# Spreading the first inversion over the preparation, in an RWKV-7 kernel with a top-k mixture behind it

## The chip, the cores and the metric

The kernel runs on one core of a Trainium2 chip. The metric is the device time of one execution in microseconds (us), as the median of several runs. The engines are TensorE (PE), VectorE (DVE), ScalarE (ACT), GpSimd (POOL) and SyncE (SP, which here only issues DMAs). Line numbers (L456) are those of the kernel before.

## The reference

Two blocks, one behind the other, in float32. The first is a recurrence over 768 time steps for 4 batches and 8 heads of 40 features:

```python
for t in range(S):
    y[:, :, t] = np.einsum('bhd,bhde->bhe', rt, state)
    Sa = np.einsum('bhde,bhe->bhd', state, at)
    state_decay = state * wt[:, :, None, :] - np.einsum('bhd,bhe->bhde', Sa, bt)
    state = state_decay + np.einsum('bhd,bhe->bhde', vt, kt)
```

The second block takes the 3072 rows of y (320 features), gives each to the best of 8 experts, keeps the 80 with the largest gate for each expert, and multiplies those by two matrices with a ReLU between.

## The kernel before, in words

**Units.** The sequence is cut into 12 chunks of 64 steps; a unit is one chunk of two batches with their eight heads, so there are 24 units. Within a chunk the recurrence is solved at once: a triangular system of 64 rows for each head and batch. Its two diagonal blocks of 32 rows are inverted explicitly; all the inversions of four units (a group) lie side by side on the 128 partitions, and one inversion handles a group.

**Preparation of a unit n**, eight units ahead of its use (`AHEAD = 8`):

- `decays` turns w on TensorE and copies it out on ACT; `forward` (L291) and `backward` (L298) are DVE's running products of it; `doubled` (L312) is a copy on POOL into `qd`.
- `turned_a` and `decayed_a` (L307) turn a on TensorE and scale it on DVE.
- `inverted` (L324, L326) turns `qd` and scales the keys and b with it on DVE: `scaled`. Behind it the next unit's keys and b are loaded into the single buffer `raw_s`.
- `operand` (L336) turns `scaled` into `sT`. `qd` and `sT` share one buffer: both are tiles of tag "turn" in a pool that has one of each tag.
- `system` (L259) multiplies `ahT` by `sT` in 64 small matmuls; `system_kept` (L346) copies the result to `nt` on ACT and writes its diagonal blocks to DRAM (`blocks`); `psi_masked` (L265) masks it on POOL.

**Inversion of a group k.** `fetch` reads the four units' blocks back in another layout (`lt`, four DMAs, L361). `begin` (L366) fills `tt` from it on POOL. Then come 30 steps (`step`, L377 and L380), each a product and a sum on DVE, of 30 to 240 elements on 128 partitions. `end` writes `tt` to DRAM (`solved`, L383), `returned` reads it back in the layout of the units (`dt`, four DMAs, L390). `diagonal` (L456) multiplies with `dt` on TensorE, twice for each unit.

**Recurrence.** The main loop has one iteration n for each unit. It finishes unit n - 1 (`turned`, `lower` with its masks on POOL, `summed`, L521, with the state update, L524), computes unit n (`together`, `right`, `diagonal` 0, `reads_g`, `below`, `turned_r`, `diagonal` 1), and prepares unit n + 8 and part of unit n + 9. The inversion of group n // 4 + 1 begins at n % 4 = 0 and its steps are spread over four iterations.

**Order.** All of this is written out by hand: `do` chains the instructions of each engine in the order of the calls, DMAs by the engine that issues them. `pause(steps, us)` emits inversion steps until their estimated costs have used up the given us. The queue for a-loads and for one of the k-loads is ACT's during the preparation, and SP's from the line `queues[1] = nc.sync` on; all other DMAs named here are SP's.

**Before the loop**, units 0 to 5 are prepared in a row, then the inversion of group 0 runs (with the rest of unit 5 beside its first steps), then units 6 and 7 are prepared and 8 is begun.

Of the kernel before, what the change touches and what calls it, by code (L numbers as in the profile page):

```python
# [8 lines left out]
F32 = mybir.dt.float32  # L9
# [9 lines left out]
def kernel(  # L19
# [32 lines left out]
    T = 64  # L52
    C = 32
    NS = T // C
    Z = 2
# [3 lines left out]
    G = H // 2  # L59
    NM = NC * BP  # L60

    NG = 4
# [83 lines left out]
    with ExitStack() as p1:  # L146
# [5 lines left out]
        sb = p1.enter_context(tc.tile_pool(name="sb", bufs=1))  # L152
# [176 lines left out]
                    in1=ps[q][:, :, :, 0:D], op=Alu.mult)  # L329
            load(n + 1, "s")  # L330

        def operand(n):
            t = sb.tile([128, G, Z, 2, T], F32, name="sT", tag="turn")
            of[n]["sT"] = sT = t.rearrange("p g z i t -> p (g z i t)").rearrange("p (z g s) -> p z g s", z=Z, g=G)
            for p, m in zip(by_half(of[n]["s"]), halves):
                nc.scalar.copy(sT[:, :, :, m], p)  # L336

# [363 lines left out]
        def pause(todo, us_):  # L701
            while todo and us_ > 0:
                cost, f = todo.pop(0)
                do(f)
                us_ -= cost

        def invert(k):
            steps.extend(((i * (C - 1 - i) * 1.04 + 155) * 2e-3, lambda i=i: step(k, i)) for i in range(1, C - 1))

        def joined(n):  # L710
            do(operand, n)
            do(system, n)
            do(system_kept, n)
            do(psi_masked, n)

        def prepare(n, before=None, next_=True):


            do(turned_a, n)
            do(decayed_a, n)  # L720
            if next_:
                do(decays, n + 1)
            if next_:
                do(forward, n + 1)
            do(inverted, n)
            if before is not None:
                do(operand, before)
                do(system, before)
                do(system_kept, before)
                do(psi_masked, before)  # L730
            if next_:
                do(backward, n + 1)
                do(doubled, n + 1)

        def started(n):
            do(decays, n)
            do(forward, n)
            do(backward, n)
            do(doubled, n)

        do(load, 0, "was")
        started(0)
        prepare(0)
        for n in range(1, NG + 1):
            prepare(n, n - 1)
        do(fetch, 0)
        do(begin, 0)
        do(load, 0, "rv")
        prepare(NG + 1, NG, False)
        invert(0)  # L750
        pause(steps, 5)
        joined(NG + 1)
        do(load, 1, "v")
        do(load, 2, "v")
        pause(steps, 100)
        do(end, 0)
        do(returned, 0)
        queues[1] = nc.sync
        started(NG + 2)
        prepare(NG + 2)  # L760
        prepare(NG + 3, NG + 2)
        prepare(NG + 4, NG + 3, False)
        do(fetch, 1)
        do(operand, NG + 4)

        waiting, turn, inverting = [], None, None

# [3 lines left out]
        for n in range(NU + 2):  # L771
# [41 lines left out]
            pause(steps, 0.4)  # L813
            if n == NU:
                pause(rounds_, 2)
            if n % NG == 0 and n + NG < NU:
                inverting = n // NG + 1
                do(begin, inverting)
                invert(inverting)
# [12 lines left out]
            if now:  # L832
                do(reads_g, n)
                do(below, n)
            pause(steps, (3.5, 5.3, 5.3, 100)[n % NG] if coming else (6.5, 9, 100, 100)[n % NG])
            pause(rounds_, LISTS.get(n, 0))
            back = None
            if inverting and not steps:
                do(end, inverting)
                back, inverting = inverting, None  # L840
# [4 lines left out]
                turn = None  # L845
            if now:
                do(turned_r, n)
            if coming and m % NG == NG - 1:
                do(fetch, m // NG)
            if back:  # L850
                do(returned, back)
            if now:
                do(reads_r, n)
                do(diagonal, n, 1)
# [225 lines left out]
```

## Time and profile before

| | us |
|---|---|
| median of 3 runs (625.06 to 629.06) | 628.08 |
| the profiled execution's own time | 625.24 |
| its span in the profile | 623.5 |
| TensorE busy / DVE / ACT / POOL | 480.9 / 370.2 / 218.4 / 187.0 |
| first step of the first inversion, end of its last | 65.25, 88.9 |
| first multiplication with `dt` (L456) | 126.84 |
| state updates of units 0 and 21 (L524) | 153.82, 482.56 |

In the timeline a row has the start, the duration, the engine and line, what is written from what, and in brackets how long the engine had been idle and what ended that. Rows of "SPq" are DMA issues, whose duration is the time that issuing takes, not that of the transfer. PEclk in the slices is the granted clock of TensorE in tenths. In the list of groups the last column is the idle time just before these instructions, with its main releaser.

### The profile page before, as it was taken

What the parts mean: (1) busy time and instruction counts of PE and PEld (TensorE: products, weight loads), DVE (VectorE), ACT (ScalarE), POOL (GpSimd) and SP (SyncE); (2) the same over time, 40 slices, a digit from 0 to 9 for tenths busy, and PEclk for the clock granted to TensorE, in tenths of its full rate; (3) what the DMA queues carried; (4) which work ended last, traced back from release to release, by engine and by line L of the source; (5) the groups of instructions that cost most, each with busy time, mean ns of one, the idle gap of its engine ahead of it and who ended that gap; (6) DMA issues with size and microseconds to landing.
All of it is one profiled execution on the core that took longest, in us unless ns stands there. A gap on an engine that the chain in (4) does not pass through costs nothing. (4 is left out here: it accounts for less than half of the span.)

```text
span 623.5 us, 25223 instructions
## 1 busy us (share of the span) xinstructions
PE 480.9 (77%) x11184; PEld 410.3 (66%) x11184; DVE 370.2 (59%) x870; ACT 218.4 (35%) x417; POOL 187.0 (30%) x277
## 2 busy tenths in 40 slices
PE   3566204797996998699988999779998830899996
PEld 2455203677885887588877788668887720787874
DVE  8533784178963698469955892587657888201010
ACT  1232201353562555455554364244554400000000
POOL 5221200223343344424444344223322210311111
PEclk9765755596997899989997799598998975899999
DMA  4646417464567455865577425335533319899500
GB/s 74 102 91 118 94 44 96 87 115 77 98 128 125 74 95 94 154 123 97 97 139 119 89 58 115 61 76 122 111 78 77 78 23 321 258 330 329 191 14 14
DMA packets 245249, 71.45 MB, mean 115 GB/s; under 512 B 229524, under 2 KB 237972, under 8 KB 245140
## 3 DMA queue, kind: packets, MB, share of 16 engines
q1 hardware_dynamic: 219888, 62.53, 47.3%
q10 hardware_dynamic: 24484, 5.67, 4.6%
q0 software_dynamic: 768, 1.64, 0.9%
q8 instruction: 88, 1.44, 0.9%
q14 instruction: 21, 0.17, 0.1%
HBM read 51.69 MB, written 18.12 MB: 112 GB/s over the span
## 5 line engine op out<-in xcount | busy, mean ns | idle before, releaser
L380 DVE TENSOR_TENSOR tt<-tt,tmp 128x30 f32<-128x30 f32 (+9 forms) x180 | 84.4, 469 | 6.6
L377 DVE TENSOR_TENSOR tmp<-tt,lt 128x30 f32<-128x30 f32 (+9 forms) x180 | 66.0, 366 | 17.4 <-POOL tt L366 6.5
L265 POOL TENSOR_SCALAR_AFFINE_SELECT side<-side 64x1024 f32<-64x1024 f32 x46 | 53.6, 1165 | 44.5 <-ACT side L507 43.0
L223 POOL COPY apart<-state 64x320 f32<-64x320 f32 x44 | 20.1, 456 | 133.2 <-DVE state L524 132.3
L456 PE MATMUL pr<-yy,dt 32*32 32x40 f32 x1536 | 42.4, 209 | 16.3 <-DMA dt<-solved 15.6
L521 PE MATMUL yp<-side,scaled 128*64 128x128 f32 (+1 forms) x768 | 51.2, 292 | 0.6 <-DVE side L505 0.6
L456 PEld LDWEIGHTS pr<-yy,dt 32*32 32x32 f32 x1536 | 35.4, 116 | 24.3 <-issue 13.5
L238 PE MATMUL tp<-ident,raw_w 128*128 128x128 f32 x96 | 18.9, 330 | 39.9 <-DMA raw_w<-in_w_dram 39.9
L521 PEld LDWEIGHTS yp<-side,scaled 128*64 128x64 f32 x768 | 45.4, 150 | 2.5 <-DVE side L505 0.9
L265 POOL TENSOR_SCALAR_AFFINE_SELECT nt<-nt 64x512 f32<-64x512 f32 x48 | 32.2, 670 | 47.4 <-ACT nt L346 45.2
L291 DVE TENSOR_TENSOR_SCAN pt<-decay,begins 128x520 f32<-128x520 f32 x24 | 32.9, 1371 | 22.0 <-ACT decay L285 20.7
L1033 DVE TENSOR_SCALAR y<-yp,weight 80x320 f32<-80x320 f32 x8 | 4.4, 547 | 70.1 <-PE yp L1031 70.1
L312 POOL COPY qd<-qt 128x1024 f32<-128x1024 f32 x24 | 24.9, 1039 | 68.2 <-DVE qt L298 60.4
L524 DVE TENSOR_TENSOR state<-yp,pt 128x320 f32<-128x320 f32 x22 | 10.8, 489 | 56.8 <-PE yp L521 56.8
L259 PE MATMUL sp<-ahT,sT 64*64 64x64 f32 x1536 | 37.5, 249 | 6.2 <-ACT sT L336 6.0
L238 PEld LDWEIGHTS tp<-ident,raw_w 128*128 128x128 f32 x96 | 13.0, 168 | 43.4 <-issue 38.9
L285 ACT COPY decay<-tp 128x512 f32<-128x512 f32 x24 | 14.1, 588 | 73.5 <-PE tp L238 64.7
L259 PEld LDWEIGHTS sp<-ahT,sT 64*64 64x64 f32 x1536 | 32.3, 159 | 10.5 <-ACT sT L336 9.4
L326 DVE TENSOR_TENSOR scaled<-raw_s,pp 128x320 f32<-128x320 f32 x48 | 21.0, 479 | 30.5 <-PE pp L324 28.5
L1031 PE MATMUL yp<-w,hT 128*80 128x320 f32 x128 | 37.4, 439 | 0.0
L414 PE MATMUL yp<-rT,gT 64*64 64x64 f32 x768 | 28.2, 223 | 11.7 <-DVE xT L530 8.8
L336 ACT COPY sT<-tp 128x512 f32<-128x512 f32 x48 | 25.8, 589 | 29.0 <-PE tp L247 25.5
(307 smaller groups left out, 1051.3 us busy)
## 6 DMA issues: line engine op xcount, KB each, us to landing
w<-in_moe_w_dram SPq DMA_DIRECT2D x8, 1280.0 KB, 14.1
w<-in_moe_w_dram SPq DMA_DIRECT2D x8, 1024.0 KB, 16.4
blocks<-nt SPq DMA_DIRECT2D x48, 128.0 KB, 2.4
raw_w<-in_w_dram SPq DMA_DIRECT2D x48, 80.0 KB, 3.3
raw_s<-in_b_dram SPq DMA_DIRECT2D x48, 80.0 KB, 3.2
raw_r<-in_r_dram SPq DMA_DIRECT2D x48, 80.0 KB, 2.9
side<-in_v_dram SPq DMA_DIRECT2D x48, 80.0 KB, 2.6
x_rows<-xb ACTq DMA_DIRECT2D x48, 80.0 KB, 2.6
```

The source lines that it names most:

```text
L238: nc.tensor.transpose(p[:, g, :], t[:, g, :], ident)
L259: nc.tensor.matmul(p[i, q, z, g, :], lhsT=lhs[m, z, g, i], rhs=rhs[m, g, halves[z]], start=True, stop=True)
L265: nc.gpsimd.affine_select(out=o, in_=o, compare_op=Alu.is_gt, fill=0.0, base=0, pattern=[[0, o.shape[1]], [1, T]], channel_multiplier=-1)
L291: nc.vector.tensor_tensor_scan(flat(pt), flat(chunks(n)), flat(begins), 0.0, op0=Alu.mult, op1=Alu.add)
L312: nc.gpsimd.tensor_copy(qd.rearrange("p g z i t -> p (g z) i t"), of[n].pop("qt")[:, :, :, 1:].rearrange("p g z t -> p (g z) t").unsqueeze ...
L336: nc.scalar.copy(sT[:, :, :, m], p)
L377: nc.vector.tensor_tensor(out=tm, in0=t3[:, 0:i, i : i + 1].to_broadcast([128, i, n]), in1=l3[:, i : i + 1, i + 1 :].to_broadcast([128, i, ...
L380: nc.vector.tensor_tensor(out=t3[:, 0:i, i + 1 :], in0=t3[:, 0:i, i + 1 :], in1=tm, op=Alu.add)
L414: yield lambda z=z, g=g, m=m: nc.tensor.matmul(y[m, z, g, 0:T], lhsT=o["gT"][m, z, g, :], rhs=o["rT"][m, g, halves[z]], start=g == 0, stop ...
L456: nc.tensor.matmul(o["pr"][m, h, :], lhsT=dt_[m, (n % NG) * 2 * G + of_head(n, h), :], rhs=o["yy"][m, h, :], start=h == 0, stop=True, skip ...
L521: nc.tensor.matmul(o["y"][m, z, g, 0 : T if last else T + HB], lhsT=o["s"][:, z, 2 * g + q, :], rhs=x, start=False, stop=True, skip_group_ ...
L1031: nc.tensor.matmul(yp, lhsT=hT[:, f, :], rhs=w2[:, f, :], start=f == 0, stop=f == FK - 1)
```

## The change

- `operand` can write `sT` to a tile of the tag "vuT", whose buffer is otherwise first used in the loop, instead of the one that it shares with `qd`. All units prepared before the loop do so.
- In `prepare`, the previous unit's `operand` moves ahead of the next unit's `forward` and ahead of `inverted`, and `pause` can emit inversion steps at two places.
- Before the loop, unit 5 and all that belongs to 4 come ahead of `begin`; the steps of the first inversion are spread over `prepare` of units 6 and 7; `end` comes ahead of unit 8's, and `returned` behind it, ahead of the second group's `fetch`. The a-loads and one of the k-loads of units 7 to 9 are issued by ACT, since `queues[1]` changes later.
- In the loop, the budgets of `pause` are 3.7, 6 and 6 instead of 3.5, 5.3 and 5.3. `end` can also be called ahead of `begin` when no steps are left, and `returned` comes ahead of `fetch` and behind `turned_r`. With these budgets all steps of groups 1 to 4 are emitted by the iteration n % 4 = 2, so that `end` and `returned` move there from n % 4 = 3.

```diff
@@ -329,9 +329,14 @@
                     in1=ps[q][:, :, :, 0:D], op=Alu.mult)
             load(n + 1, "s")
 
-        def operand(n):
-            t = sb.tile([128, G, Z, 2, T], F32, name="sT", tag="turn")
-            of[n]["sT"] = sT = t.rearrange("p g z i t -> p (g z i t)").rearrange("p (z g s) -> p z g s", z=Z, g=G)
+        def operand(n, shared=True):
+            if shared:
+                t = sb.tile([128, G, Z, 2, T], F32, name="sT", tag="turn")
+                sT = t.rearrange("p g z i t -> p (g z i t)").rearrange("p (z g s) -> p z g s", z=Z, g=G)
+            else:
+
+                sT = sb.tile([128, Z, G, 128], F32, name="vuT", tag="vuT")
+            of[n]["sT"] = sT
             for p, m in zip(by_half(of[n]["s"]), halves):
                 nc.scalar.copy(sT[:, :, :, m], p)
 
@@ -707,61 +712,52 @@
         def invert(k):
             steps.extend(((i * (C - 1 - i) * 1.04 + 155) * 2e-3, lambda i=i: step(k, i)) for i in range(1, C - 1))
 
-        def joined(n):
-            do(operand, n)
-            do(system, n)
-            do(system_kept, n)
-            do(psi_masked, n)
-
-        def prepare(n, before=None, next_=True):
-
+        def prepare(n, before=None, next_=True, us_=0):
 
             do(turned_a, n)
             do(decayed_a, n)
             if next_:
                 do(decays, n + 1)
+            if before is not None:
+                do(operand, before, False)
             if next_:
                 do(forward, n + 1)
+            pause(steps, us_)
             do(inverted, n)
             if before is not None:
-                do(operand, before)
                 do(system, before)
                 do(system_kept, before)
                 do(psi_masked, before)
             if next_:
                 do(backward, n + 1)
                 do(doubled, n + 1)
-
-        def started(n):
-            do(decays, n)
-            do(forward, n)
-            do(backward, n)
-            do(doubled, n)
+            pause(steps, us_)
 
         do(load, 0, "was")
-        started(0)
+        do(decays, 0)
+        do(forward, 0)
+        do(backward, 0)
+        do(doubled, 0)
         prepare(0)
         for n in range(1, NG + 1):
             prepare(n, n - 1)
         do(fetch, 0)
+        prepare(NG + 1, NG)
         do(begin, 0)
+        invert(0)
         do(load, 0, "rv")
-        prepare(NG + 1, NG, False)
-        invert(0)
-        pause(steps, 5)
-        joined(NG + 1)
+        pause(steps, 3)
+        prepare(NG + 2, NG + 1, us_=4)
         do(load, 1, "v")
         do(load, 2, "v")
+        prepare(NG + 3, NG + 2, us_=4)
         pause(steps, 100)
         do(end, 0)
+        prepare(NG + 4, NG + 3, False)
         do(returned, 0)
         queues[1] = nc.sync
-        started(NG + 2)
-        prepare(NG + 2)
-        prepare(NG + 3, NG + 2)
-        prepare(NG + 4, NG + 3, False)
+        do(operand, NG + 4, False)
         do(fetch, 1)
-        do(operand, NG + 4)
 
         waiting, turn, inverting = [], None, None
 
@@ -813,6 +809,10 @@
             pause(steps, 0.4)
             if n == NU:
                 pause(rounds_, 2)
+            back = None
+            if inverting and not steps:
+                do(end, inverting)
+                back, inverting = inverting, None
             if n % NG == 0 and n + NG < NU:
                 inverting = n // NG + 1
                 do(begin, inverting)
@@ -832,9 +832,8 @@
             if now:
                 do(reads_g, n)
                 do(below, n)
-            pause(steps, (3.5, 5.3, 5.3, 100)[n % NG] if coming else (6.5, 9, 100, 100)[n % NG])
+            pause(steps, (3.7, 6, 6, 100)[n % NG] if coming else (6.5, 9, 100, 100)[n % NG])
             pause(rounds_, LISTS.get(n, 0))
-            back = None
             if inverting and not steps:
                 do(end, inverting)
                 back, inverting = inverting, None
@@ -845,10 +844,10 @@
                 turn = None
             if now:
                 do(turned_r, n)
+            if back:
+                do(returned, back)
             if coming and m % NG == NG - 1:
                 do(fetch, m // NG)
-            if back:
-                do(returned, back)
             if now:
                 do(reads_r, n)
                 do(diagonal, n, 1)
```

## The prediction

> **What bounds the kernel now.** I read the slices first, then the costliest groups, then the timeline at the two places they point to. The chain that ended last is of no use here: it covers only the last 18 us.
>
> ```profile
> PE   3566204797996998699988999779998830899996
> ...
> DVE  8533784178963698469955892587657888201010
> ...
> PEclk9765755596997899989997799598998975899999
> ...
> L456 PE MATMUL pr<-yy,dt 32*32 32x40 f32 x1536 | 42.4, 209 | 16.3 <-DMA dt<-solved 15.6
> ...
> L238 PE MATMUL tp<-ident,raw_w 128*128 128x128 f32 x96 | 18.9, 330 | 39.9 <-DMA raw_w<-in_w_dram 39.9
> ```
>
> A slice is 15.6 us. TensorE stands almost still in slices 5 and 6 (62 to 94 us), between the preparation and the recurrence; nearly all of L238's 39.9 us is one wait of 31.1 us there. L456, the multiplication with the inverses, waits 15.6 us for their arrival.
>
> The timeline of one prepared unit in the old order:
>
> ```profile
> 46.44 1.04 POOL L312 COPY qd<-qt 128x1024 f32<-128x1024 f32 x1
> ...
> 47.54 1.12 PE L324 MATMUL pp<-ident,qd 64*128 64x64 f32 x16 [1.77 <-POOL qd L312]
> ...
> 50.37 1.07 ACT L336 COPY sT<-tp 128x512 f32<-128x512 f32 x2 [3.30 <-PE tp L247]
> ...
> 51.01 2.46 PE L259 MATMUL sp<-ahT,sT 64*64 64x64 f32 x64 [0.66 <-ACT sT L336]
> ...
> 53.52 1.01 ACT L346 COPY nt<-sp 128x1024 f32<-128x1024 f32 x1 [2.07 <-PE sp L259]
> ...
> 54.60 1.38 POOL L265 TENSOR_SCALAR_AFFINE_SELECT nt<-nt 64x512 f32<-64x512 f32 x2 [7.11 <-ACT nt L346]
> ...
> 56.04 1.04 POOL L312 COPY qd<-qt 128x1024 f32<-128x1024 f32 x1
> ```
>
> Each step releases the next, round a ring of 9.4 us a unit (the scores of units 0, 1, 2 begin at 22.68, 32.05 and 41.41). `qd` and `sT` share one buffer, so the ring takes in DVE's `scaled`, the turning of the operand and its copies. Then comes the hole:
>
> ```profile
> 66.89 0.60 PE L238 MATMUL tp<-ident,raw_a 128*128 128x128 f32 x4
> ...
> 88.68 0.21 DVE L380 TENSOR_TENSOR tt<-tt,tmp 128x30 f32<-128x30 f32 x1
> ...
> 91.63 2.18 SPq L390 DMA_DIRECT2D dt<-solved  x4
> ...
> 98.63 1.09 PE L238 MATMUL tp<-ident,raw_w 128*128 128x128 f32 x4 [31.14 <-DMA raw_w<-in_w_dram]
> ```
>
> For 23.6 us only DVE works, on the first inversion; units 6 and 7 are prepared after it. The first use of `dt` is at 126.84. In the loop, at unit 4:
>
> ```profile
> 181.65 0.57 SPq L383 DMA_DIRECT2D solved<-tt  x1
> ...
> 184.04 4.08 SPq L361 DMA_DIRECT2D lt<-blocks  x4
> 188.16 3.02 SPq L390 DMA_DIRECT2D dt<-solved  x3
> ...
> 192.57 0.23 PE L456 MATMUL pr<-yy,dt 32*32 32x40 f32 x2 [3.15 <-DMA dt<-solved]
> 194.31 1.27 PE L456 MATMUL pr<-yy,dt 32*32 32x40 f32 x30 [1.51 <-DMA dt<-solved]
> ```
>
> `dt` is issued behind `lt`, and TensorE stands for it. State updates (L524) date the iterations: 169.62, 182.94, 208.13, 224.07, 239.18, 253.15, 274.54. The iterations of n = 4, 8, 12 and 16 take 25.2, 21.4, 20.0 and 20.7 us, the others mostly 12 to 16. Those of n%4 = 1 and 2 are DVE's: its state update follows inversion steps without a wait.
>
> **The change, part by part.**
>
> *Own buffer for the operand, turned before `inverted`.* Out of the ring go `scaled`, 16 transposes and two copies. Left are qd 1.04, its transposes 1.12, scores 2.46, nt 1.01 and masks 1.38 = 7.0, with five hand-overs of some 0.06 as in the rows: 7.3 us. The ring next in line is `raw_s`: issued from 15.21, it released `scaled` at 20.39, with 0.9 for `scaled` 6.1 us. ACT's (a-loads 1.49, decay 0.59, sT 1.07, k-load 0.64, nt 1.01 = 4.8) and TensorE's sum (four groups of 1.1, scores 2.46 = 6.9) lie below 7.3. The scores of unit 0 no longer wait for `scaled` of unit 1 and can start at 18.7; those of 1 wait for the nt copy behind a k-load (26.6), then 7.2 each: unit 3 at 41.0, against 51.01. **10 us earlier**, and so the four `lt` fetches and `begin`: 63.95 becomes 54, the first step 55.3.
>
> These are half-rate durations. The page "TensorE: Matmul & The Clock Gate" (Part 4) says transposes don't bring up the full clock, which would hold all of this at half rate. The row in the loop, 16 transposes in 0.71 instead of 1.12 at a granted clock of 1.00, shows them at full rate beside dense matmuls. If the denser preparation gets it, `raw_s` binds at 6.1 and some 4 us more are won. I take half rate, as the preparation rows show, and keep the 4 us for the range.
>
> *Inversion spread.* The 60 steps took 23.6 us (65.25 to 88.9). In their first 4.18 us POOL worked 2.69 us and DVE's pairs ran 1.6 us longer than their sizes ask, 0.6 us for 1 of POOL; so 22.0 alone. Two units' DVE work now lies among them: ahT 0.67, pt 1.24, scaled 0.87, ends 0.20, qt 1.24 = 4.2, twice 8.4. Two units' POOL work (1.38 + 1.04) is 4.8, at 0.6 another 2.9. The page "SBUF — State Buffer" (two separate sides) calls the pair of ports that DVE and GpSimd share an exclusive lock, the loser waiting fully, for DVE operations with two SBUF inputs: that speaks against the spreading and would charge 4.8. The row decides: 2.9, with 1.9 kept for the range. 22.0 + 8.4 + 2.9 = 33.3: the steps end at 88.6, **as before**, but with units 6 and 7 beside them.
>
> Behind a step on DVE's queue now stand ahT and scaled of units 6 to 8; ACT's nt copy and POOL's masks wait for them through the k-load. No harm: a unit has 12 us of DVE work there, and the other rings need 7.3.
>
> *What follows the last step.* ahT of unit 8 frees its PSUM bank (0.7); transposes, scores of 7 and nt copy 4.8 with hand-overs; two `blocks` issues 1.2: 95.2. `solved` (4.3 to land) is in by 93. Four `dt` issues end at 97.9, the last lands 3.9 after its start: 101.2. TensorE gets there with operand 8, scores 8 and unit 0's first products at about the same time. So 126.84 becomes 101.3: **25 us earlier**. The moved a- and k-loads leave SP for ACT (2.1 a unit), covered by its 4.8 of 7.3; r and v issues (5.5 on SP) lie beside the steps. `lt` of the second group is issued at 98 and lands at 102, 1 us after the first use of `dt`; before it was 4.
>
> *The loop: 3.7, 6, 6 instead of 3.5, 5.3, 5.3.* DVE's changed order has steps 18 to 30 before the state update of n%4 = 2; before it was 18 to 27, the rest in n%4 = 3. That is 0.7 us more for a DVE-bound iteration, 0.1 in n%4 = 1: four groups, **+3 us**. In n%4 = 3 DVE had 4 to 5 us to spare.
>
> *`end` and `returned` one iteration earlier.* On SP: `solved` (one), r (two), then `dt` (four) with the wait for `solved`, and behind it v, w, blocks, a, s, r and `lt`. Counted from the state update of n = 2: solved lands +4.3, dt issued to +7, v +8.4, w +9.7, blocks +11, a +12.4, s +15, r +16.4, `lt` +19 to +20.5, landed +24. At n = 4 (it starts +13.3) `dt` is long there, w lands about +13, a +16, s +20: on time, with less than 1 us to spare for w. But `begin` waits for `lt`, and behind it on POOL stand the masks that `summed` needs and, on DVE, eight pairs of steps ahead of the state update: +24 + 1.4 + 4.8 = +30.2. So n = 4 takes 16.8, not the 14 that its TensorE work asks: 25.2 - 16.8 = 8.4. With 14 us for n = 7 and 11: 21.4 - 16.2 = 5.1 and 20.0 - 16.4 = 3.7. At n = 16 no more w, a, s are loaded, `lt` lands as now, and eleven pairs end at 402 against 405.9: 4. Sum **-21 us**. The last group's `end` stays where it was.
>
> The dt waits (4.7 us) were followed by half-rate passes to 207.9 (L521 3.31 for 1.97). The same clock page ("Why this matters for your kernels") puts the limit at an idle gap of about 3 us; my remaining wait is 1 to 3. If it does drop the clock, 1.5 to 3 us come back at three boundaries.
>
> **Sum:** -25 + 3 - 21 = -43 on the profiled execution's 625.24, 582.2, a factor of 0.931. On the median of 628.08 that is **585 us**.
>
> **Rivals.** (1) *Half of it*: the wait for `dt` becomes one for `lt` of the same length, so only some 4 of the 21 remain. For: the SP count above. Against: `lt` now lands only 2 us later than it did. -25 + 3 - 4 = -26: 602. A preparation tied up by its three PSUM banks, gaining 10 for 25, gives 600. (2) *More*: full clock in the preparation (4 more) and `lt` in time for TensorE (31 for 21): -57, 571. For: SP's issue rows are often 0.65 each. Against: PEclk 0.5 to 0.7 there. (3) *Slower*: `lt`, at the end of an SP queue held by `solved`'s landing, comes far later, since w, blocks, a and s wait in turn for engines that wait for them. Each us costs one at n = 4, 8, 12: from 14 us beyond my +24 the gain is gone; at 20 beyond, 60 - 43 = 17: 645. Against: no wait in the list is circular, and all that is ahead of `lt` takes 16.4 of some 27 us. (4) *No change*: needs both gains gone; the 31 us hole speaks against it.
>
> **Numbers.** Forecast (about 575 to 597) 0.50, half 0.23, more 0.19, no change 0.03, slower 0.05. Range 566 to 606: from the case of more to the half case, each with some 4 us for the spread of runs (and, above, for the lock's charge). Within 1% (the three runs lie 0.6% apart) 0.03; faster 0.92, slower 0.05.
>
> **What would show it.** Scores of unit 3 near 41; steps from 55 to 89; no TensorE gap over 6 us between; first `dt` use near 101; L456's wait for `dt` near nothing; n = 4 near 17 us with POOL waiting for `lt`; n%4 = 2 longer by 0.7. First `dt` use after 115, or boundaries still over 20, would make me wrong.

## The result, and the profile after

| | before | after |
|---|---|---|
| median of the runs, us | 628.57 (625.06 to 633.86) | **599.63** (594.01 to 609.03) |
| ratio, 95% interval | | **0.950** [0.940, 0.961] |
| state update of unit 0 | 153.82 | 124.20 |
| from there to the state update of unit 21 | 328.74 | 332.05 |
| iterations n = 4, 8, 12, 16 | 25.2, 21.4, 20.1, 20.7 | 23.1, 23.8, 23.8, 18.5 |
| TensorE's wait for `dt` in all | 15.6 | 2.6 |
| POOL's wait for `lt` in all | 15.8 | 38.8 |

585 was forecast, with a range of 566 to 606: faster, as forecast, but by 5% and not by 7%. The whole gain lies before the loop; the loop, where 18 us of the 43 were expected, is 3.3 us longer. Ratios compare fast executions only, and stages only up to the state update of unit 21, because the profiled executions of after, e4, e7 and e9 were slow ones, which took 151 to 153 us behind that point at a granted clock of 0.82 to 0.83, where all the others took 140 to 142 at 0.88 to 0.90. "The state update of n" below is the one that iteration n makes, for unit n - 1, and the time that an iteration takes is that from the state update before to its own. Lines from 335 on are five higher in after than in before: L461 is the old L456, L526 the old L521, L529 the old L524.

From the page of after, the slices (of 15.2 us) and two of the costliest groups:

```profile
PE   3865458988878895989868986889988416999996
...
PEclk9976667899979988899989889789999757589999
...
L526 PE MATMUL yp<-side,scaled 128*64 128x128 f32 (+1 forms) x768 | 50.5, 289 | 16.4 <-POOL side L265 15.8
...
L461 PE MATMUL pr<-yy,dt 32*32 32x40 f32 x1536 | 38.1, 201 | 4.2 <-DMA dt<-solved 2.6
```

TensorE's hole in slices 5 and 6 (digits 2 and 0 before) is half filled (4 and 5), slice 7 is at 8 instead of 4, and L461 hardly waits for the inverses any more. In its place L526, the product with the masked `side`, waits 15.8 us for POOL, four times: as long as L456 waited before.

The timeline of after, one unit of the preparation:

```profile
31.03 1.08 ACT L341 COPY vuT<-tp 128x512 f32<-128x512 f32 x2
31.81 1.12 PE L324 MATMUL pp<-ident,qd 64*128 64x64 f32 x16 [1.52 <-POOL qd L312]
32.86 1.98 PE L259 MATMUL sp<-ahT,vuT 64*64 64x64 f32 x64
...
34.91 1.02 ACT L351 COPY nt<-sp 128x1024 f32<-128x1024 f32 x1 [2.79 <-PE sp L259]
35.99 1.37 POOL L265 TENSOR_SCALAR_AFFINE_SELECT nt<-nt 64x512 f32<-64x512 f32 x2 [4.23 <-ACT nt L351]
...
37.43 1.04 POOL L312 COPY qd<-qt 128x1024 f32<-128x1024 f32 x1
```

The ring is the one that was forecast: masks, `qd`, its transposes, scores, `nt` and masks again, without the operand and `scaled`. It takes 6.6 us (scores at 26.34, 32.86, 39.57), mainly because the scores last 1.98 instead of 2.46. The timeline of after, the end of the first inversion:

```profile
54.13 0.19 DVE L382 TENSOR_TENSOR tmp<-tt,lt 128x30 f32<-128x30 f32 x1 [5.40 <-POOL tt L371]
...
86.14 0.22 DVE L385 TENSOR_TENSOR tt<-tt,tmp 128x30 f32<-128x30 f32 x1
86.42 0.35 SPq L388 DMA_DIRECT2D solved<-tt  x1
...
90.12 1.22 SPq L354 DMA_DIRECT2D blocks<-nt  x2
91.44 3.55 SPq L395 DMA_DIRECT2D dt<-solved  x4
...
97.79 0.76 PE L461 MATMUL pr<-yy,dt 32*32 32x40 f32 x30 [2.06 <-DMA dt<-solved]
```

The steps end 2 us earlier than before although two units are prepared beside them. The first multiplication with all of `dt` is at 97.8 instead of 126.84.

The timeline of after at the boundary n = 4; the state update of n = 2 lies at 139.98:

```profile
140.14 0.35 SPq L388 DMA_DIRECT2D solved<-tt  x1
...
143.22 2.68 SPq L395 DMA_DIRECT2D dt<-solved  x4
...
149.45 1.22 SPq L354 DMA_DIRECT2D blocks<-nt  x2
154.80 1.34 SPq L201 DMA_DIRECT2D raw_a<-in_a_dram  x2
...
161.44 3.41 SPq L366 DMA_DIRECT2D lt<-blocks  x4
...
168.52 1.26 POOL L371 TENSOR_SCALAR_AFFINE_SELECT tt<-lt 128x1024 f32<-128x1024 f32 x1 [8.71 <-DMA lt<-blocks]
...
169.91 2.34 POOL L265 TENSOR_SCALAR_AFFINE_SELECT side<-side 64x1024 f32<-64x1024 f32 x2
170.05 1.04 DVE L385 TENSOR_TENSOR tt<-tt,tmp 128x30 f32<-128x30 f32 x1
171.12 1.20 DVE L382 TENSOR_TENSOR tmp<-tt,lt 128x58 f32<-128x58 f32 x1
172.31 3.68 PE L526 MATMUL yp<-side,scaled 128*64 128x128 f32 x32 [4.26 <-POOL side L265]
172.32 1.36 POOL L265 TENSOR_SCALAR_AFFINE_SELECT nt<-nt 64x512 f32<-64x512 f32 x2
...
177.51 0.48 DVE L529 TENSOR_TENSOR state<-yp,pt 128x320 f32<-128x320 f32 x1
```

`solved` and `dt` are out early, as forecast. But behind the `blocks` SP issues nothing for 4.1 us (150.67 to 154.80); `lt` follows the loads for a, s and r, and POOL stands 8.7 us for it with the masks behind it. `begin` comes 28.5 us behind the state update of n = 2, not 24. Then POOL's masks run beside the first steps, and a sum over 30 elements lasts 1.04 us where the same row at 86.14 shows 0.22. What held SP is in its waits (DMA queue of SP in after; us in all, times, longest), and POOL's and TensorE's waits stand beside it:

```profile
SPq L201 <- DMA x_rows<-xb: 20.2, 10, 4.1
...
POOL tt L371 <- DMA lt<-blocks: 38.8, 6, 8.7
...
PE yp L526 <- POOL side L265: 15.8, 4, 5.7
```

The load of a waited for the landing of `x_rows`, a write of the mixture's rows that ACT issues at 152.57 and 153.12. The two have no data in common. What they share is a semaphore: the trace names the one that tells of each landing, and all DMAs of SP and ACT together take eight of them in turn, in program order. The load at 154.80 has the same one as the write at 152.57, eight places before it, which landed at 154.74.

### The profile page after: what moved, and what is told of

Read it like the earlier page. It is cut to its first block, busy times and chain, and to the rows that moved or that the text cites. A ratio compares the mean times of both kernels' runs of the same rounds, so it can differ in the third digit from the quotient of the medians.

```text
span 607.2 us, 25214 instructions
## 1 busy us (share of the span) xinstructions
PE 480.3 (79%) x11184; PEld 411.6 (68%) x11184; DVE 372.6 (61%) x870; ACT 217.6 (36%) x417; POOL 186.6 (31%) x277
## 5 line engine op out<-in xcount | busy, mean ns | idle before, releaser
L382 DVE TENSOR_TENSOR tmp<-tt,lt 128x30 f32<-128x30 f32 (+9 forms) x180 | 72.1, 400 | 35.1 <-POOL tt L371 25.1
L385 DVE TENSOR_TENSOR tt<-tt,tmp 128x30 f32<-128x30 f32 (+9 forms) x180 | 80.9, 449 | 6.6
L526 PE MATMUL yp<-side,scaled 128*64 128x128 f32 (+1 forms) x768 | 50.5, 289 | 16.4 <-POOL side L265 15.8
L526 PEld LDWEIGHTS yp<-side,scaled 128*64 128x64 f32 x768 | 44.6, 148 | 18.4 <-POOL side L265 16.3
L223 POOL COPY apart<-state 64x320 f32<-64x320 f32 x44 | 19.9, 452 | 110.8 <-DVE state L529 109.9
L419 PE MATMUL yp<-rT,gT 64*64 64x64 f32 x768 | 29.3, 228 | 25.2 <-DVE xT L535 23.7
L419 PEld LDWEIGHTS yp<-rT,gT 64*64 64x64 f32 x768 | 26.7, 143 | 26.8 <-issue 23.7
L461 PE MATMUL pr<-yy,dt 32*32 32x40 f32 x1536 | 38.1, 201 | 4.2 <-DMA dt<-solved 2.6
L461 PEld LDWEIGHTS pr<-yy,dt 32*32 32x32 f32 x1536 | 31.8, 109 | 11.0 <-issue 6.2
L351 ACT COPY nt<-sp 128x1024 f32<-128x1024 f32 x24 | 24.3, 1011 | 38.5 <-PE sp L259 13.6
L1013 PEld LDWEIGHTS hp<-xe,w 128*128 128x128 f32 x256 | 36.2, 227 | 1.5 <-DVE xe L1005 0.2
L1013 PE MATMUL hp<-xe,w 128*128 128x80 f32 x256 | 36.4, 311 | 0.0
L529 DVE TENSOR_TENSOR state<-yp,pt 128x320 f32<-128x320 f32 x22 | 10.7, 486 | 40.9 <-PE yp L526 40.9
L1024 ACT ACTIVATE hT<-hp 128x320 f32<-128x320 f32 x16 | 6.1, 435 | 82.0 <-PE hp L1020 82.0
L326 DVE TENSOR_TENSOR scaled<-raw_s,pp 128x320 f32<-128x320 f32 x48 | 21.1, 481 | 21.8 <-PE pp L324 13.2
```

The costliest lines, as they stand in the source:

```text
L326: nc.vector.tensor_tensor(out=s[:, :, :, 0:D].rearrange("p z (g q) d -> p z g q d", q=2)[:, :, :, q, :], in0=raw["s"][0].rearrange("p z (g ...
L351: nc.scalar.copy(nt.rearrange("p z (q g) t -> p q z (g t)", q=2), p.rearrange("p q z g t -> p q z (g t)"))
L382: nc.vector.tensor_tensor(out=tm, in0=t3[:, 0:i, i : i + 1].to_broadcast([128, i, n]), in1=l3[:, i : i + 1, i + 1 :].to_broadcast([128, i, ...
L385: nc.vector.tensor_tensor(out=t3[:, 0:i, i + 1 :], in0=t3[:, 0:i, i + 1 :], in1=tm, op=Alu.add)
L419: yield lambda z=z, g=g, m=m: nc.tensor.matmul(y[m, z, g, 0:T], lhsT=o["gT"][m, z, g, :], rhs=o["rT"][m, g, halves[z]], start=g == 0, stop ...
L461: nc.tensor.matmul(o["pr"][m, h, :], lhsT=dt_[m, (n % NG) * 2 * G + of_head(n, h), :], rhs=o["yy"][m, h, :], start=h == 0, stop=True, skip ...
```

## The experiments

All are edits of after, e2 of before. In the table "start" is the state update of unit 0, "loop" the time from there to that of unit 21, in the profiled execution; the kernel before, run beside them, took 630.0 to 631.8 us.

| | us (range) | ratio to before | start | loop | n = 4, 8, 12 |
|---|---|---|---|---|---|
| before | 628.57 | 1 | 153.8 | 328.7 | 25.2, 21.4, 20.1 |
| after | 599.63 | 0.950 [0.940, 0.961] | 124.2 | 332.1 | 23.1, 23.8, 23.8 |
| e1 preparation only | 602.95 (598.29 to 605.06) | 0.958 [0.950, 0.967] | 124.8 | 330.3 | 23.7, 26.4, 21.2 |
| e2 loop only | 625.54 (621.94 to 635.39) | 0.994 [0.988, 0.999] | 152.2 | 329.0 | 21.9, 23.7, 23.1 |
| e3 early fetch | 579.79 (579.48 to 588.68) | 0.920 [0.910, 0.931] | 124.9 | 311.8 | 16.7, 17.2, 19.0 |
| e4 return held | 600.34 (589.27 to 608.42) | 0.940 [0.928, 0.952] | 125.1 | 330.7 | 23.2, 20.7, 22.4 |
| e5 own buffer only | 602.36, 615.02 | | 129.7 | 330.2 | 22.2, 24.6, 24.0 |
| e6 spread only | 611.52, 626.63 | | 140.9 | 327.8 | 22.6, 23.1, 24.2 |
| e7 x_rows by SP | 598.15 (590.09 to 606.16) | 0.946 [0.935, 0.957] | 126.2 | 326.8 | 19.3, 20.2, 20.0 |
| e8 end with fetch | **577.70** (575.44 to 586.52) | 0.922 [0.913, 0.930] | 125.0 | 308.3 | 16.2, 16.3, 16.4 |
| e9 masks first | 591.32 (589.36 to 602.36) | 0.939 [0.931, 0.947] | 125.8 | 322.0 | 20.8, 21.6, 20.4 |
| e10 e8 and e7 | 580.20 (575.90 to 587.31) | 0.920 [0.911, 0.929] | 123.3 | 309.8 | 16.0, 19.9, 15.7 |
| e11 e8 and e9 | 580.16 (577.80 to 583.32) | 0.923 [0.915, 0.930] | 123.0 | 315.6 | 17.6, 19.6, 18.4 |

### e1 and e2: the two parts alone

e1 takes the loop's edits back; e2 makes only them, in before:

```diff
# e1, against after
-            back = None
-            if inverting and not steps:
-                do(end, inverting)
-                back, inverting = inverting, None
             if n % NG == 0 and n + NG < NU:
...
-            pause(steps, (3.7, 6, 6, 100)[n % NG] if coming else (6.5, 9, 100, 100)[n % NG])
+            pause(steps, (3.5, 5.3, 5.3, 100)[n % NG] if coming else (6.5, 9, 100, 100)[n % NG])
...
-            if back:
-                do(returned, back)
             if coming and m % NG == NG - 1:
                 do(fetch, m // NG)
+            if back:
+                do(returned, back)
```

> Only the part before the loop is changed; in the loop the budgets, end, returned and fetch stand as before. Theory A (all of the gain was made ahead of the loop, where the state update of unit 0 comes 29.6 us earlier, and the loop's edits gave back some 3 us): about 597 us, up to 3 us below the changed kernel; state updates of units 0 and 21 near 124 and 453. Theory B (the loop's edits gained as predicted, and the part before the loop less): about 610 us or more.

> Only the loop is changed; the part before it stands as before. Theory A: no gain, 628 to 632 us, the iterations of n = 4, 8, 12 still 20 to 24 us long but now waiting for lt instead of dt. Theory B: 18 us less than before, about 610 us.

The preparation alone brings nearly everything (0.958), the loop's edits alone next to nothing (0.994): e1's gain of 4.2% and e2's of 0.6% add up to after's 5.0%, within the intervals. (e1 was expected at 597 and took 602.95; by its interval it is not told from after.) In e1 the start is at 124.8, and TensorE waits 16.4 us for `dt`, as it did before (15.6). In e2 this wait is gone, but POOL waits 38.6 us for `lt` and TensorE 14.2 for the masks behind it. So the loop's part does what it says, and the wait for `dt` is turned into one for `lt` with or without the new preparation.

### e5 and e6: the parts of the preparation

e5 keeps the operand's own buffer and the new order, and emits all steps of the first inversion at once. e6 keeps the spreading, and puts the operand back on the shared buffer and behind `inverted`.

```diff
# e5
-        pause(steps, 3)
-        prepare(NG + 2, NG + 1, us_=4)
-        do(load, 1, "v")
-        do(load, 2, "v")
-        prepare(NG + 3, NG + 2, us_=4)
         pause(steps, 100)
         do(end, 0)
+        prepare(NG + 2, NG + 1)
+        do(load, 1, "v")
+        do(load, 2, "v")
+        prepare(NG + 3, NG + 2)
# e6
-            if before is not None:
-                do(operand, before, False)
...
             if before is not None:
+                do(operand, before)
                 do(system, before)
...
-        do(operand, NG + 4, False)
+        do(operand, NG + 4)
```

> The changed kernel with the steps of the first inversion not spread: all 30 pairs and end stand ahead of the preparation of unit 6; operand keeps its own buffer and its new place. Theory A (shorter rings in the preparation carry most of the gain ahead of the loop: 10 us for units 0 to 3, and as much again for units 6 to 8, whose ring of 9.4 us becomes one of 6.5 to 7): state update of unit 0 at 128 to 132, about 605 us. Theory S (the spreading, which fills the TensorE hole of 31 us, carries it): near 144 (only the first 10 us are won), about 619 us.

> The changed kernel with operand back on the buffer that it shares with qd and behind inverted, everything else as changed, the steps spread over units 6 and 7. Theory A: first step near 64 instead of 54, state update of unit 0 near 135 to 138 (16 to 19 of the 29.6 us are won): about 612 us. Theory S: state update of unit 0 within 3 us of the changed kernel's 124, about 601 us.

Of the 29.6 us by which the start comes earlier, e5 has 24.2 (129.67) and e6 12.9 (140.94). The two overlap: taken behind the own buffer and the order, the spreading brings 5.5 us; taken behind the spreading, the buffer and the order bring 16.7. (e5's start lies in the range expected for it, e6's comes 3 us later than its range.) In e5 the first steps begin right behind `begin` at 52.7 and `solved` is written at 76.1, 10 us earlier than in after, but `dt` is issued only at 96.7, as units 6 and 7 are prepared behind the steps. In e6 the scores still follow each other at 9.6 us (41.37, 50.96, 60.55, each 2.46 long and released by the copy of `sT`), so that `begin` comes at 66.6. With two runs each, their totals say no more than that both lie between before and after.

### e3, e4 and e8: where on SP's queue `lt` stands

e3 leaves `end` where after has it (n % 4 = 2), but issues the return and the fetch right behind the `blocks` of the next iteration, ahead of its loads of a, s and r. e4 also ends early, but returns behind the fetch, with the fetch in its old place (`owed` starts as None in both):

```diff
# e3
                 do(system_kept, m)
+            if coming and m % NG == NG - 1:
+                if owed:
+                    do(returned, owed)
+                    owed = None
+                do(fetch, m // NG)
...
-            if back:
+            if back and coming:
+                owed = back
+            elif back:
                 do(returned, back)
-            if coming and m % NG == NG - 1:
-                do(fetch, m // NG)
# e4
-            if back:
-                do(returned, back)
             if coming and m % NG == NG - 1:
                 do(fetch, m // NG)
+                if owed:
+                    do(returned, owed)
+                    owed = None
+            if back and coming:
+                owed = back
+            elif back:
+                do(returned, back)
```

> The changed kernel, with returned held from n%4 = 2 to n%4 = 3 and set, with fetch behind it, right behind that iteration's blocks, ahead of the loads of a, keys and r. Theory A (lt is late because it stands last in an SP queue that was held up first for solved and then for x_rows): lt lands about 15 us after the state update of n%4 = 2 instead of 28, n = 4, 8 and 12 take 16 to 17 us instead of 23 to 24, n = 16 some 4 us less: about 578 us. Theory B (the boundary is long for DVE's or TensorE's own work, whatever lt does): 597 to 600 us.

> The changed kernel, with end left at n%4 = 2 but returned held until behind fetch in n%4 = 3. The wait for solved no longer holds SP. Theory A: lt lands 6 to 8 us earlier than in the changed kernel, but dt now stands behind it and lands about when it is needed: n = 4, 8, 12 take 18 to 20 us, about 588 to 592 us. Theory B: 597 to 600 us.

The timeline of e3 at n = 4:

```profile
148.26 3.42 SPq L395 DMA_DIRECT2D dt<-solved  x4
151.73 4.93 SPq L366 DMA_DIRECT2D lt<-blocks  x4
...
160.83 1.26 POOL L371 TENSOR_SCALAR_AFFINE_SELECT tt<-lt 128x1024 f32<-128x1024 f32 x1
...
169.14 1.97 PE L526 MATMUL yp<-side,scaled 128*64 128x128 f32 x32
...
172.23 0.49 DVE L529 TENSOR_TENSOR state<-yp,pt 128x320 f32<-128x320 f32 x1
```

Counted from the state update of n = 2 (here at 141.54), `lt` is issued at 10.2 us instead of 21.5, `begin` has no wait in its row, L526 runs without a wait at full rate (1.97 instead of 3.68), and n = 4 takes 16.7 us. The loop is 20 us shorter. The only thing changed is the place of eight issues on SP's queue, so that place is the cause. (n = 8 takes 17.2 in e3, but n = 12 takes 19.0: there TensorE stands 2.97 us, until 287.62, for the load of a, which SP issued behind the eight.)

e4 was expected to bring half of this, with 18 to 20 us for n = 4, 8 and 12; they take 20.7 to 23.2, and by its interval it is not told from after. Its timeline at n = 4:

```profile
155.30 2.95 SPq L366 DMA_DIRECT2D lt<-blocks  x4
158.30 4.37 SPq L395 DMA_DIRECT2D dt<-solved  x4
...
163.38 0.23 PE L461 MATMUL pr<-yy,dt 32*32 32x40 f32 x2 [0.96 <-DMA dt<-solved]
165.38 1.27 PE L461 MATMUL pr<-yy,dt 32*32 32x40 f32 x30 [1.77 <-DMA dt<-solved]
```

Now `lt` is in time and `dt` is late, as in before: TensorE waits 18.6 us for `dt` in the whole run, and from this wait on it runs at half rate (1.27 for 30 multiplications that take 0.76 at 97.79 of after). Eight issues of 0.7 to 1.2 us each (means of four) stand on one queue, and both groups of four are needed at the same boundary: ahead of the a-, s- and r-loads both are in time (e3), behind them the second is late.

e8 takes e3's order further. It has the old budgets, so the last steps fall into n % 4 = 3 again, and `end`, the fetch and the return are issued together at once behind the last of them:

```diff
# e8
                 back, inverting = inverting, None
+                if coming:
+                    assert m % NG == NG - 1
+                    do(fetch, m // NG)
+                    do(returned, back)
+                    back = None
             if n % NG == 0 and n + NG < NU:
...
-            pause(steps, (3.7, 6, 6, 100)[n % NG] if coming else (6.5, 9, 100, 100)[n % NG])
+            pause(steps, (3.5, 5.3, 5.3, 100)[n % NG] if coming else (6.5, 9, 100, 100)[n % NG])
...
-            if coming and m % NG == NG - 1:
-                do(fetch, m // NG)
```

> The changed kernel with the old budgets 3.5, 5.3, 5.3; the last steps fall into n%4 = 3 as before the change, and end, fetch and returned follow them at once there, ahead of the loads of keys and r. Against the run with returned and fetch right behind the blocks (580 us), three pairs of steps (some 0.7 us net) leave the DVE-bound iteration n%4 = 2, and lt lands some 1 to 2 us later, still ahead of begin: 576 to 580 us if DVE's work in n%4 = 2 counts fully. If the early end is what makes the boundary short, n = 4, 8, 12 are back at 19 us or more and it takes 588 or more.

At 577.70 us it is faster than both kernels (ratio to before 0.922, its interval below after's), and it is not told from e3. The timeline of e8 at n = 4:

```profile
148.72 0.35 SPq L388 DMA_DIRECT2D solved<-tt  x1
149.17 3.38 SPq L366 DMA_DIRECT2D lt<-blocks  x4
152.65 4.33 SPq L395 DMA_DIRECT2D dt<-solved  x4
...
169.50 1.97 PE L526 MATMUL yp<-side,scaled 128*64 128x128 f32 x32
...
171.58 0.49 DVE L529 TENSOR_TENSOR state<-yp,pt 128x320 f32<-128x320 f32 x1 [1.17 <-PE yp L526]
```

The four `lt` issues fill the time in which `solved` lands, so `dt` has nothing to wait for. The state update waits for TensorE here, not for the steps. In this iteration (155.3 to 171.6) TensorE's granted clock is 1.00; in after's n = 4 it is 0.87, in before's 0.73. So ending the steps one iteration earlier isn't needed for this: what counts is that both groups of issues stand ahead of the s-loads.

### e7 and e9: what made `lt` and the steps late in after

e7 has SP issue the `x_rows` writes, so that no load of SP's waits for a write that ACT issues. e9 leaves `lt` late and puts `begin` and the steps behind the masks:

```diff
# e7
-                nc.scalar.dma_start(x_dram[row : row + T, :]...
+                nc.sync.dma_start(x_dram[row : row + T, :]...
# e9
-            if n % NG == 0 and n + NG < NU:
-                inverting = n // NG + 1
-                do(begin, inverting)
-                invert(inverting)
             if past:
                 do(lower, o)
             if coming:
                 do(psi_masked, m)
+            if n % NG == 0 and n + NG < NU:
+                inverting = n // NG + 1
+                do(begin, inverting)
+                invert(inverting)
```

> The changed kernel with the two writes of x_rows of each unit issued by SP instead of ACT, in the same place of the program. In the built program SP's and ACT's DMAs take eight completion semaphores in turn, and an issue waits for the one eight before it. If SP's wait of 4 us for x_rows in n%4 = 3 delays lt, lt lands 3 us earlier (4 saved, 1.2 for the issue) and n = 4, 8, 12 are 3 us shorter each: about 590 us. If lt's place in the queue and the wait for solved alone make it late: 600 us or a little more, for the issue time added to SP.

> The changed kernel with one thing moved: at n%4 = 0 `begin` and the new steps come behind `lower` and `psi_masked` in every engine's order, so that POOL makes the masks of the side matrices while it would otherwise stand waiting for `lt`. The landing of `lt` is left as late as it is (27 to 28 us behind the state update of n = 2). Theory A (of the 23 to 24 us of n = 4 and 8, about 3 us are the eight pairs stretched beside POOL's masks and TensorE's wait for the masks; the rest is the late `lt`): n = 4, 8 and 12 take about 20.2, the eight pairs 4.8 to 5.2 us instead of 7.7, no wait of TensorE on the side masks of L265 above 1 us at a boundary; the loop from state update 0 to 21 about 321 us instead of 332; total 588 to 592. Theory B (the steps were not stretched by the masks but by something else, such as the products of the step itself, and the iteration ends with the steps anyway): the periods stay at 23 to 24, total about 599.

The timeline of e7 at n = 4, with the state update of n = 2 at 142.0:

```profile
153.07 1.22 SPq L354 DMA_DIRECT2D blocks<-nt  x2
154.38 1.62 SPq L201 DMA_DIRECT2D raw_a<-in_a_dram  x2
...
160.80 3.56 SPq L366 DMA_DIRECT2D lt<-blocks  x4
...
166.85 1.26 POOL L371 TENSOR_SCALAR_AFFINE_SELECT tt<-lt 128x1024 f32<-128x1024 f32 x1 [4.98 <-DMA lt<-blocks]
```

The 4 us between the `blocks` and the load of a are gone, no wait of SP's loads on `x_rows` is left in its waits, and `begin` comes 24.9 us behind the state update of n = 2 instead of 28.5: **3.7 us** of the lateness were this, though SP now issues the writes as well (2.1 us at 149.41). The eight turns are those that after's trace showed; now the write stands on SP's own queue, well ahead of the load that takes its semaphore. The iterations n = 4, 8 and 12 are 3.6 to 3.8 us shorter, but the total is not told from after's (ratios 0.946 and 0.950): only 5 us of this are left in the loop, and ACT now waits 19.9 us for the landing of these writes (L556) where it did not.

The timeline of e9 at n = 4:

```profile
163.70 2.35 POOL L265 TENSOR_SCALAR_AFFINE_SELECT side<-side 64x1024 f32<-64x1024 f32 x2 [2.68 <-ACT side L512]
...
169.05 1.97 PE L526 MATMUL yp<-side,scaled 128*64 128x128 f32 x32
170.05 1.26 POOL L371 TENSOR_SCALAR_AFFINE_SELECT tt<-lt 128x1024 f32<-128x1024 f32 x1 [2.58 <-DMA lt<-blocks]
171.35 0.19 DVE L382 TENSOR_TENSOR tmp<-tt,lt 128x30 f32<-128x30 f32 x1 [5.27 <-POOL tt L371]
...
171.57 0.19 DVE L385 TENSOR_TENSOR tt<-tt,tmp 128x30 f32<-128x30 f32 x1
...
176.30 0.48 DVE L529 TENSOR_TENSOR state<-yp,pt 128x320 f32<-128x320 f32 x1
```

`lt` is as late as in after (`begin` 28.5 us behind the update of n = 2), but the masks are made meanwhile. TensorE has no wait and runs at full rate, and the eight pairs take 5.0 us (171.35 to 176.3) instead of 7.7 (169.82 to 177.5). n = 4, 8 and 12 take 20.8, 21.6 and 20.4, where 20.2 were expected; the loop is 10 us shorter. So **2.7 us** at the boundary were the masks beside the steps.

### e10 and e11: the same two edits in e8

> The kernel of e8 (end, fetch and return at once after the last steps in n%4 = 3, the old budgets) with the x_rows writes issued by SP instead of ACT, as in e7. Theory A (in e8 `lt` no longer sets the end of the boundary iterations, so the 7 us that SP waits in all on the x_rows writes cost nothing): within 1% of e8, 574 to 582, the periods of n = 4, 8 and 12 still 16.2 to 16.5. Theory B (SP's waits still delay a, s or r loads that TensorE needs): 3 boundaries shorter by 1 to 2 us each, 570 to 574. A loss is possible too: SP gets 22 more issues of some 0.6 us; if these delay the loads, above 582.

> The kernel of e8 with `begin` and the new steps behind `lower` and `psi_masked`, as in e9. In e8 `lt` has landed before `begin`, so POOL doesn't stand for it; its copy into tt (1.3 us) only stands ahead of the masks. Theory A (the masks reach TensorE 1.3 us earlier at n = 4, 8 and 12, and the eight pairs start later by the 3.7 us of the masks but run unstretched; TensorE's product with the side matrices ends these iterations): n = 4, 8 and 12 take 15 to 16 us, total 574 to 578, not told from e8. Theory B (the steps, now starting behind the masks, end the iterations instead): 17 to 18 us each, total 579 to 583.

Neither is told from e8 by its total (580.20 and 580.16). In e10 SP's waits on `x_rows` are gone and the loop is no shorter (309.8 against 308.3), but n = 8 takes 19.9 us instead of 16.3. The timeline of e10 there shows the edit's own price:

```profile
228.07 0.45 ACT L556 COPY xb<-xp__4219 128x352 f32<-128x352 f32 x1 [4.22 <-DMA x_rows<-xb]
...
228.58 0.87 PE L247 MATMUL tp<-ident,scaled 64*128 64x64 f32 x16 [2.39 <-ACT xb L556]
```

ACT now stands for a write that is issued late on SP's busy queue (at 224.07), and TensorE for ACT. At n = 4 and 12 the iterations are 0.2 and 0.7 us shorter than in e8. So SP's waits on `x_rows` cost little where `lt` is in time; that they cost nothing isn't shown. In e11 the steps start only behind the masks (`begin` at 165.1 instead of 160.65) and then end n = 4: the three boundaries take 17.6, 19.6 and 18.4 us, the dearer of the two cases that were written down or more, and the loop is 7 us longer. The place that helps when `lt` is late hurts when it is in time.

## Why the prediction was right or wrong

**Right: the preparation, somewhat better than its sum.** The ring was forecast at 7.3 us and is 6.6; unit 3's scores, forecast at 41.0, are at 39.57. The term that was off is the scores: 2.46 us in the sum, 1.98 here. It was read as a duration at half rate, but it has a wait in it. In before the scores started behind the first of the two `sT` copies and stood for the second. The weight loads (PEld) of the scores at 51.01 show it; the first four come at 51.01, the other 60 behind that copy:

```profile
51.49 1.79 PEld L259 LDWEIGHTS sp<-ahT,sT 64*64 64x64 f32 x60 [0.20 <-ACT sT L336]
```

In after both copies are done before the scores begin. The rate is the same: one of the 64 multiplications takes 311 ns at 51.01 of before and at 32.86 of after, and 218 ns at full rate (unit 1 of after, 1.16 us for all).

The clock was left open between a row of the loop and the Trainium skill's page "TensorE: Matmul & The Clock Gate" (Part 4), which says that transposes don't bring up the full clock. In after it alternates from unit 2 on, within each turn of the ring. Two stretches of 3.41 us; the numbers behind that are the busy us of TensorE, its weight loads, DVE, ACT and POOL, and the third from the end is the granted clock:

```profile
31.59:35.00 3.41, 3.19 (x81) 2.96 (x82) 2.68 (x5) 0.62 (x3) 0.17 (x1) 0.50 0.73 150
35.00:38.41 3.41, 1.78 (x24) 1.27 (x23) 1.81 (x3) 1.94 (x4) 2.29 (x3) 1.00 0.81 143
```

The transposes of `qd` and the scores fall into the half-rate stretch (1.12 and 1.98), the transposes of the raw tiles and of `scaled` into the other (16 in 0.71 at 36.54). So transposes run at whatever rate is granted; whether they alone would bring it up, no run here shows. Over 30 to 50 us the mean granted clock is 0.74, against 0.59 before, but the full-rate stretches hold no TensorE work of the ring itself, and the 4 us held back for a full clock did not come.

The first step is at 54.13 (55.3 forecast), and the steps with two units beside them take 32.2 us (33.3). The lock rule of the skill's page "SBUF — State Buffer" (two separate sides) charged 1.9 more, 35.2; the row's 0.6 us for each of POOL's was nearer. Six steps of these rows were stretched, by 2.8 us in all, beside 5.1 us of POOL's (the last section shows how).

What the prediction had less well is which part earns it: 10 us for the buffer and the order, the rest for the spreading. e5 has 24.2 us without any spreading, which adds 5.5: the shorter ring also serves units 6 to 8.

**Right in kind, 4 us short: what follows the last step.** 101.3 was forecast for the first use of `dt`, 97.8 came. The `blocks` of unit 7 were put at 94 to 95.2, behind the transposes and scores of unit 7, worked out as if these began after the last step. They run beside the last steps (scores at 84.80), and `blocks` are issued at 90.12. So -25 became -29.6 at the first state update.

**Right: the budgets.** +3 us was forecast; n = 2, 6, 10 and 14 are longer by 0, 0.7, 1.1 and 1.4, in all 3.2.

**Wrong: the loop boundaries, -21.** n = 4, 8, 12 and 16 together change by -2.1 + 2.4 + 3.7 - 2.2 = +1.8 us: they lose. (All iterations but these and n = 2, 6, 10 and 14 are 1.7 us shorter together.) Three of the four lie over 20 us, which the prediction had named as a sign of being wrong. The step that failed is the line "+24 + 1.4 + 4.8 = +30.2", and two of its three terms did:

- *+24 for the landing of `lt`.* It was counted from the SP issues alone, each released in time by its own data. Without the write of ACT's it nearly holds: e7 gives 24.9, with 2.1 us of issues in it that the count did not have. In after 3.7 us come on top, in which SP stands on that write. The waits of SP on `x_rows` were in the profile of before too, 10.5 us in four waits, up to 4.0 each; I left them out of the count.
- *4.8 for the eight pairs.* These are durations of steps that run alone. The masks of `lower` and `psi_masked`, 3.7 us of POOL, stand right behind `begin` on POOL, so a late `begin` puts them beside the first steps: 7.7 us. The prediction named these masks as what waits behind `begin`, and charged POOL's work beside DVE in the first inversion, but not here.

For n = 4 the sum closes. The state update was put 30.2 us behind that of n = 2; 0.9 for the rest of the landing, 3.7 for the write of ACT's and 2.8 for the stretched pairs make 37.6, and 37.5 were measured. The iteration n = 3 in between took 14.5 us instead of 13.3, so 23.1 are left for n = 4. e9, without the stretched pairs, takes 20.4 to 21.6 at the three boundaries, e7, without the write, 19.3 to 20.2; a kernel with both edits was not run. (That e3 takes 16.7 at n = 4, close to the predicted 16.8, is chance: its `lt` is early, so it shows another limit.)

**The clock at the boundary.** 1.5 to 3 us for a dropped clock were kept in the range. The drop is there: behind the wait of 4.26 us L526 takes 3.68 us instead of 1.97. At n = 4 it cost nothing, since the steps ended after it; where TensorE's side comes last, as in e4, it does.

**The rival that came.** "Half of it: the wait for `dt` becomes one for `lt`" was put at 602, and 599.6 were measured. The mechanism is this rival's: 15.6 us of waiting for `dt` became 15.8 us of waiting for the masks behind `lt`. That the total agrees so well is partly luck: the rival left 4 us of the boundaries' gain where there was a loss of 2, and the preparation gave 4.6 more than in its sum. The reason given against it, that "`lt` now lands only 2 us later than it did", fails in its number: counted from the state update of n = 2, `lt` landed at 21.6 us in before (its `begin` at 21.8) and at 28.4 in after, 7 us later. And the iteration was to end earlier, so that even 2 us count. The total lies in the range because the range reached to this rival's case; it lies outside the 575 to 597 of the forecast itself.

## What to carry to other kernels

Moving a transfer ahead on an in-order DMA queue moves everything behind it back: list what falls behind it, with the time it is needed at in the new, shorter schedule, before counting the gain. A wait that looks harmless in the old profile, like SP's on `x_rows`, belongs in the count as soon as the queue comes onto the path. And a small instruction on an engine's queue that can be late, like `begin`, should stand behind the work that is ready (e9), unless the late data can be made early (e8), which is better.

## What the runs showed of the hardware

- POOL's masks beside DVE's steps, which read two SBUF operands: each of POOL's instructions let just one step through, which began during it and ended 0.04 to 0.27 us behind it. Beside the four masks from 169.91 on in after (1.14, 1.14, 0.65 and 0.66 us) four steps of 0.19 to 0.25 took 1.04, 1.20, 0.68 and 0.70. What this costs is POOL's time less the steps' own: 2.7 us for 3.6 here, 2.8 for 5.1 in after's first inversion (steps of 0.73, 0.73 and 1.13 at 67.06, 67.83 and 68.60 instead of 0.41), 1.6 for 2.7 in that of before. The share of 0.6 to 0.7 holds for steps as short as these.
- The granted clock changes on a grid: in all 13 traces every stretch of one clock lasts 3.41 us or a multiple of it (leaving out the last one of each trace). Over the stretches of 3.41 us of these traces, full followed on half 164 times, and TensorE had been busy in at least 84% of the stretch before each; half followed on full 177 times, behind at most 75% each. Of the stretches at full clock, those under 46% were all followed by half; between 46% and 75% both occur. These are shares of modelled matmul times, and not every stretch that was busy throughout was followed by the full clock.
- So several short gaps can drop the clock, and the drop comes late. In e4 gaps of 0.84, 0.96 and 1.77 us within 160.2 to 165.4 went with a drop at 164.3, and half rate lasted to 177.9. In after, gaps of 0.53 and 2.06 us ahead of 97.79 left the next multiplications at full rate (0.76 us), but from 99.9 to 110.1 the granted clock was 0.50 (the 32 multiplications at 102.69 took 1.28).
- All DMAs of SP and ACT took eight completion semaphores in turn, so that a load waited up to 4.1 us for a write of the other queue that it shares no data with (ten waits of 20.2 us in after, none of SP's loads in e7).
